# Batch 0 of a fused Fourier mixing and gated FFN kernel: even row sets summed as two 64-row tiles over half the columns

## The chip, the cores and the metric

The kernel runs on one core of one Trainium2 chip, in a single launch. The metric is the device time of that launch in microseconds (us), as a median of several runs. The engines are named as the profile names them: PE is TensorE's matmul and PEld its weight load, DVE is VectorE, ACT is ScalarE, POOL is GpSimd, and SP is SyncE, which here does nothing but issue DMA transfers. Each engine works through its own instructions in order.

## What is computed

```python
# x: (8, 3008, 256) float32; w_gate, w_val: (256, 1536); w_out: (1536, 256), given as float64
X = np.fft.fft(x, axis=1)              # along the sequence
X = np.fft.fft(X, axis=2)              # along the features
x = X.real.astype(np.float32).reshape(8 * 3008, 256)
gate = 1.0 / (1.0 + np.exp(-(x @ w_gate)))
val = x @ w_val
out = (gate * val @ w_out).astype(np.float32)
```

The real part of the two transforms is a cosine sum along the sequence times a cosine sum along the features, minus the same with sines. The feature transform is a fixed matrix, so the kernel multiplies it into w_gate and w_val once ("merge"), which gives the two halves G1 and G2. What is left per batch is a cosine sum pk and a sine sum qk along the sequence, for the outputs k = 0 to 1504. Row k of the output uses G1 pk + G2 qk, and row 3008 - k uses G1 pk - G2 qk.

## The kernel before, in words

**Rows and tables.** With S = 3008 and M = 1504, the input xf holds for each s from 0 to 767 the four rows s, S - s, M + s and M - s. s is p * 6 + q, where p is the partition (128 of them) and q = 0 to 5 is a "row set"; so the parity of s is the parity of q. The table stab holds the weighted cosines (t = 0) and sines (t = 1) of 2 pi s k / S in the same layout. Its columns are the even k from 0 to 752 (NE = 377 of them) and then the odd k (NO = 376); the two kinds of columns are "blk" 0 and 1.

**Folds.** `fold_ops` (L487) adds and subtracts the four rows of each s on DVE until each blk has 128 features for the cosine sum and 128 for the sine sum. For batch 0 it works in four slices of row sets, (0, 1), (2, 3), (4), (5) (L485), each with seven DVE instructions, L494 to L583.

**Sums.** `half` (L595), through `seq_group` (L680), makes one of the four groups (cosine or sine, blk 0 or 1). For each q a matmul with the folded rows as weights and 377 or 376 table columns adds into one of two PSUM banks: ev for even q, od for odd q. When all six are done, ACT copies ev to SBUF (L607), and `places` (L611) writes ev + od to the places of k and ev - od to those of M - k, one DVE instruction each (L613, L617). In the trace each float32 matmul is two instructions, so "x2" is one.

**The single feature column e.** Feature 128 has no partner in the fold. `e_sums` (L696) sums this column separately, for batch 0 during the start and for the other seven batches later from the tile x8. `e_load` (L684) fills x8 with one transfer for each of batches 1 to 7, issued at the main loop's steps 21 to 27; `e_fold` and `e_joint` use it at steps 36 to 44. Results go to the DRAM tile ed and come back as broadcast rows ek (`e_rows`, L755), from which ACT seeds the PSUM banks of the main loop (`seed`, L772). The ek row for steps 36 to 47 is issued at step 25.

**Weights.** Each of 18 pieces is loaded as float64 (`weight_load`, L328, 512 KB). ACT splits it (`weight_parts`, L382 and L383), DVE (`weight_join`, L392 to L395) and POOL (L397) put float32 numbers together, and `weight_use` either stores the piece or merges it: `merge` (L410) is four matmuls into one PSUM bank "ps" and two copies by ACT (L417, L418). Pieces 0 and 1, the first of w_gate and of w_val, have to be merged before the main loop.

**Main loop.** 576 steps (L1151) run over 8 batches, 6 chunks of up to 252 outputs k, and 12 blocks of 128 hidden features. `front_a` multiplies G1 with pk and `front_b` G2 with qk, into banks "pf"; ACT and DVE form the gates; POOL forms sums of gate blocks ("sf"), and `back` multiplies by the output weights into banks "po". Side work of later batches (loads, folds, tables) hangs on step numbers through lists such as `at(i, f)`. The table loads for batches 1 to 7 (`quarter_load`, L247) go to 32 partitions each.

**Order.** The order of instructions on each engine is the order in which the Python code issues them; nothing is reordered. All loads of the start go through SP's queue, in the order of L954 to L971. The start of batch 0 stands at L973 to L1015:

```python
    for q, f in zip(SLICES, fold_ops(0, 2), strict=True):
        f()
        e_(*{1: (0, 1), 5: (2, 3, 4, 5)}.get(q[-1], ()))
        sin[0][0](*{5: (3,)}.get(q[-1], ()))
        cos[0][0](*q)
        cos[1][0](*q)
        sin[0][0](*{1: (0, 1), 4: (2,), 5: (4, 5)}.get(q[-1], ()))
```

PSUM has eight banks: `bank(name)` takes one of three that rotate, `bank(name, i)` one of five named po0 to po4.

Of the kernel before, what the change touches and what calls it, by code (L numbers as in the profile page):

```python
# [8 lines left out]
F32 = mybir.dt.float32  # L9
# [3 lines left out]
ALU = mybir.AluOpType  # L13
# [40 lines left out]
NQ = 6  # L54
NP = 128
HP = 64
# [25 lines left out]
def kernel(  # L82
# [10 lines left out]
    nc = tc.nc  # L93
    B, _, _, _, D = xf.shape
    F = moe_w_gate.shape[1]
    P = 128
# [3 lines left out]
    NE = (M // 2) // 2 + 1  # L100
    NO = (M // 2) // 2
# [3 lines left out]
    CH = 252  # L105
    NB = 1 + max(b // 3 for b in PLACE)
    WC = 256
    HD = D // 2
# [23 lines left out]
    def mm(o, l, r, start, stop):  # L132
        nc.tensor.matmul(o, l, r, start=start, stop=stop, skip_group_check=True)  # L133
# [55 lines left out]
    ed = dram.tile([B, NK + 1], F32, name="ed")  # L189

    def load_rows(q, n):
        nc.sync.dma_start(out=X[0][0:NP, :, q : q + n], in_=xf[0, :, :, q : q + n])  # L192

    def load_table(t, q, n, lo=0, hi=NE + NO):
        nc.sync.dma_start(out=ST[t][0:NP, q : q + n, lo:hi], in_=stab[:, t, q : q + n, lo:hi])

    NQ4 = NE // 4 + 1
    TILES = [(g, par, par * HP + g * TB) for g in range(2) for par in range(2)]
# [178 lines left out]
    def weight_parts(j):  # L377

        if j in RAW:
            raw, ws = RAW[j], WS[j]  # L380
            lo, hi = raw[:, :, :, 0], raw[:, :, :, 1]
            nc.scalar.activation(ws, hi.bitcast(F32), AF.Abs)  # L382
            nc.scalar.activation(lo, lo.bitcast(U32), AF.Copy, scale=2.0 ** -29)  # L383

    def weight_join(j):
        if j not in RAW:
            return
        raw, ws = RAW.pop(j), WS[j]
# [8 lines left out]
        nc.gpsimd.tensor_tensor(wi, wi, lo, op=ALU.add)  # L397
# [5 lines left out]
    def weight_use(j):  # L403
        w, c = jobs[j]
        if w == 2:
            WO[c] = WS.pop(j)
        else:
            merge(WS.pop(j), w, c, (4, 2, 3)[next(turns) % 3] if j > 1 else None)

    def merge(ws, g, c, other):  # L410
        cs = slice(c * WC, (c + 1) * WC)
        ps = bank("ps", other)
# [179 lines left out]

    PQE = {}

    def half(b, w, d, blk, sn, other=None):  # L595


        c0, n = ((0, NE), (NE, NO))[blk]
        ev, od = [bank(name, other and other[i])[:, 0:n] for i, name in enumerate(("ev", "od"))]

        def sums(*qs):
            for q in sorted(qs, key=lambda q: q % 2):
                mm((ev, od)[q % 2], w(q), ST[int(sn)][0:NP, q, c0 : c0 + n], q < 2, q >= NQ - 2)

        def then():
            a = evp.tile([P, NE], F32, name="a", tag="a")[:, 0:n]
            nc.scalar.copy(a, ev)  # L607
            return lambda: places(d, blk, sn, a, od)
        return sums, then

    def places(d, blk, sn, ev, od, ends=(0, 1)):  # L611
        if 0 in ends:
            nc.vector.tensor_tensor(d[:, blk : blk + 2 * ev.shape[1] - 1 : 2], ev, od, op=ALU.add)  # L613
        lo, hi = (od, ev) if sn else (ev, od)
        top = M - blk
        if 1 in ends:
            nc.vector.tensor_tensor(d[:, top : top - 2 * NO + 1 : -2], lo[:, 0:NO], hi[:, 0:NO],  # L617
                                    op=ALU.subtract)
# [58 lines left out]
        for t in PQE[b]:  # L677
            nc.vector.memset(t[:, NK:], 0.0)

    def seq_group(b, blk, what, other=None):  # L680
        return half(b, lambda q: W[b, blk][what][:, q, :], PQE[b][what], blk, what == 1, other)


    def e_load(b):  # L684
        nc.sync.dma_start(out=x8[:, b - 1], in_=xf[b, :, :, :, HD : HD + 1])

    def e_fold():
        tt = nc.gpsimd.tensor_tensor
# [7 lines left out]
    def e_sums(m=B - 1):  # L696


        ps = bank("pe", NB - 1)
# [252 lines left out]
    nc.gpsimd.dma_start(out=zero, in_=nil)  # L952
    nc.scalar.dma_start(out=dt, in_=dtab.rearrange("(c p) d -> p c d", p=P))
    load_x(0)  # L954
    for j in range(2):
        weight_load(j)
    load_rows(0, 2)
    load_table(0, 0, 2)
    load_rows(2, 2)
    load_table(1, 0, 2, 0, NE)  # L960
    load_table(0, 2, 2)
    load_rows(4, 1)
    load_table(0, 4, 1)
# [12 lines left out]
    weight_parts(1)  # L976
    weight_join(0)
    weight_join(1)
# [5 lines left out]
    seq_start(0)  # L984

    cos = [seq_group(0, blk, 0, (2 * blk, 2 * blk + 1)) for blk in range(2)]
    e_, e_even = e_sums(1)
    sin = [seq_group(0, 0, 1)]
    for q, f in zip(SLICES, fold_ops(0, 2), strict=True):
        f()  # L990
        e_(*{1: (0, 1), 5: (2, 3, 4, 5)}.get(q[-1], ()))
        sin[0][0](*{5: (3,)}.get(q[-1], ()))
        cos[0][0](*q)
        cos[1][0](*q)
        sin[0][0](*{1: (0, 1), 4: (2,), 5: (4, 5)}.get(q[-1], ()))
    places_c = [cos[blk][1]() for blk in range(2)]
    weight_parts(2)
    weight_join(2)
    rest, *ends = e_even()
    rest()  # L1000
    for f in ends:
        f()
    for f in places_c:
        f()
    nc.scalar.copy(e0[0:1], E0[0][:, 0:CH])
    weight_parts(3)
    weight_join(3)
    sin.append(seq_group(0, 1, 1, (0, 1)))
    sin[1][0](*range(NQ))
    for j in range(KEEP, KEEP + 3):  # L1010
        weight_load(j)
    places_s = [group[1]() for group in sin]
    for f in places_s:
        f()
    e_rows(0)  # L1015

    per = NFT * len(chunks)
# [2 lines left out]
    def at(i, *fs):  # L1020
        side.setdefault(i, []).extend(fs)
# [224 lines left out]
```

## Time and profile before

| what | value |
|---|---|
| median of 3 runs | 1909.21 us (1908.49 to 1910.1) |
| the profiled execution | 1909.15 us, its span 1907.4 us |
| PE, DVE, POOL, ACT busy | 99%, 80%, 81%, 71% of the span |
| granted PE clock | 1.00 |
| DVE's folds of batch 0 | 10.18 to 24.61 us |
| first sum of the main loop (pf) | 33.05 us |
| last SP issue of an e_load | ends at 163.35 us |
| bytes moved by DMA | 109.33 MB, 315 GB/s in the first fortieth of the span |

A line of a timeline reads: start in us, time in us, engine, line of the code, operation, output<-inputs, shapes, number of instructions, and in brackets how long the engine had been idle and what released it. SPq is SP's queue; an SPq line is the time that the issue of a transfer took, not the transfer. A line of the table by windows gives, for each stretch, the busy time of PE, PEld, DVE, ACT and POOL with the number of instructions, then the granted clock, the mean busy share of the 16 DMA engines and what they moved in GB/s.

### The profile page before, as it was taken

How to read it: one execution, taken by the hardware profiler on the slowest of the kernel's cores; microseconds unless marked ns; L12 is line 12 of the kernel's file. 1: busy time of each engine (PE TensorE's matmuls, PEld its weight loads, DVE VectorE, ACT ScalarE, POOL GpSimd, SP SyncE). 2: the span in 40 equal slices, each digit the busy share in tenths (PEclk: the TensorE clock that was granted, in tenths of full speed). 3: DMA queues.
4: the chain of work that ended last, by engine and by line, in shares of the span. 5: the costliest groups of instructions: out<-in, count | busy, mean ns of one | idle time of the engine just before them, and what ended most of it. 6: DMA issues, size and time to landing. Idle time of an engine off the chain costs nothing.

```text
span 1907.4 us, 36057 instructions
## 1 busy us (share of the span) xinstructions
PE 1895.6 (99%) x11836; PEld 1756.6 (92%) x11836; DVE 1520.6 (80%) x3375; ACT 1353.2 (71%) x3235; POOL 1543.4 (81%) x2733
## 2 busy tenths in 40 slices
PE   8999999999999999999999999999999999999999
PEld 5788999999999999999999999999999999999998
DVE  7678888878979778897788878888788777977775
ACT  4777777777777777777777777677767777777775
POOL 2489879987999779997799878999789986877770
PEclk9999999999999999999999999999999999999999
DMA  8446221212022121211211212122120110010001
GB/s 315 120 134 80 71 89 51 72 33 81 21 64 54 31 87 32 62 41 37 89 39 48 45 39 81 40 52 58 30 74 17 36 37 15 15 25 17 15 18 30
DMA packets 197333, 109.33 MB, mean 57 GB/s; under 512 B 134823, under 2 KB 188818, under 8 KB 195354
## 3 DMA queue, kind: packets, MB, share of 16 engines
q1 hardware_dynamic: 196568, 106.50, 21.1%
q8 instruction: 95, 1.56, 0.3%
q14 instruction: 92, 0.75, 0.1%
q10 hardware_dynamic: 546, 0.51, 0.1%
q0 software_dynamic: 32, 0.00, 0.0%
HBM read 71.24 MB, written 47.87 MB: 62 GB/s over the span
## 4 chain that ended last, share of the span: by engine, by line
PE 94%; DMA 2%; SPq 1%; POOL 1%; ACT 1%; DVE 0%; issue 0%; ACTq 0%; POOLq 0%
PE pf L133 49%; PE po L133 41%; PE sum L133 2%; DMA rtab<-in_stab_dram 1%; PE ps L133 1%; POOL sf L824 1%; DMA st<-in_stab_dram 1%; SPq L206 1%; DMA raw<-in_moe_w_val_dram 0%; PE od L133 0%; POOL x L507 0%; SPq L192 0%; SPq L375 0%; PE pe L133 0%; PE ev L133 0%
## 5 line engine op out<-in xcount | busy, mean ns | idle before, releaser
L824 POOL TENSOR_TENSOR sf<-h,sf 128x168 f32<-128x168 f32 (+1 forms) x1104 | 621.0, 582 | 79.5 <-DVE h L818 75.9
L824 POOL TENSOR_TENSOR sf<-h 128x168 f32<-128x168 f32 (+1 forms) x920 | 519.3, 584 | 159.8 <-DVE h L818 158.0
L133 PE MATMUL pf<-qk,G 128*128 128x252 f32 (+1 forms) x2304 | 583.4, 376 | 0.9 <-ACT ae L787 0.8
L133 PE MATMUL pf<-pk,G 128*128 128x252 f32 (+1 forms) x2304 | 582.7, 376 | 0.0
L772 ACT ACTIVATE pf<-ek,ge 128x252 f32<-128x252 f32 (+1 forms) x1142 | 538.2, 471 | 23.2 <-DMA ge<-G 3.0
L133 PE MATMUL po<-sf,wf 128*128 128x168 f32 (+1 forms) x2944 | 508.3, 305 | 0.0
L787 ACT ACTIVATE ae<-pf 128x504 f32<-128x504 f32 (+1 forms) x576 | 338.8, 588 | 218.7 <-PE pf L133 217.2
L133 PEld LDWEIGHTS pf<-pk,G 128*128 128x128 f32 x2304 | 435.9, 190 | 53.3 <-ACT pf L772 1.5
L133 PE MATMUL po<-h,wf 128*128 128x168 f32 (+2 forms) x2584 | 461.3, 307 | 0.0
L133 PEld LDWEIGHTS po<-sf,wf 128*128 128x128 f32 x2944 | 453.4, 190 | 8.0
L818 DVE TENSOR_TENSOR h<-pf,z 128x252 f32<-128x252 f32 (+1 forms) x576 | 240.4, 417 | 274.0 <-ACT pf L815 270.5
L802 DVE TENSOR_TENSOR z<-ae,pf 128x504 f32<-128x504 f32 (+1 forms) x576 | 384.6, 668 | 83.1 <-ACT h L801 79.1
L908 DVE TENSOR_TENSOR c<-c 128x168 f32<-128x168 f32 (+1 forms) x920 | 438.7, 500 | 3.3
L133 PEld LDWEIGHTS pf<-qk,G 128*128 128x128 f32 x2304 | 410.6, 190 | 32.3 <-ACT ae L787 2.1
L133 PEld LDWEIGHTS po<-h,wf 128*128 128x128 f32 x2584 | 410.4, 190 | 17.8 <-issue 0.9
L801 ACT ACTIVATE h<-pf 128x252 f32<-128x252 f32 (+1 forms) x576 | 216.9, 376 | 146.3 <-PE pf L133 129.0
L815 ACT ACTIVATE pf<-z 128x252 f32<-128x252 f32 (+1 forms) x576 | 214.3, 372 | 116.4 <-DVE h L814 114.5
L814 DVE TENSOR_TENSOR h<-h,pf 128x252 f32<-128x252 f32 (+1 forms) x576 | 232.9, 404 | 0.0
L824 POOL TENSOR_TENSOR sf<-sf 128x168 f32<-128x168 f32 (+1 forms) x184 | 101.7, 553 | 14.4
L824 POOL TENSOR_TENSOR sf<-sf,h 128x168 f32<-128x168 f32 (+1 forms) x184 | 110.1, 598 | 0.0
L891 ACT COPY c<-po 128x504 f32<-128x504 f32 (+1 forms) x138 | 78.5, 569 | 0.0
L918 DVE STREAM_TRANSPOSE os<-c 128x256 f32<-128x256 f32 x188 | 76.5, 427 | 0.1
(158 smaller groups left out, 876.4 us busy)
## 6 DMA issues: line engine op xcount, KB each, us to landing
x<-xr SPq DMA_DIRECT2D x14, 1536.0 KB
out_dram<-os SPq DMA_DIRECT2D x376, 56.0 KB
xr<-in_xf_dram SPq DMA_DIRECT2D x105, 128.0 KB
x<-x SPq DMA_DIRECT2D x112, 96.0 KB
xr<-in_xf_dram SPq DMA_DIRECT2D x14, 384.0 KB
ek<-ed SPq DMA_DIRECT2D x40, 126.0 KB
out_dram<-os SPq DMA_DIRECT2D x288, 7.0 KB
xr<-in_xf_dram SPq DMA_DIRECT2D x21, 124.0 KB
```

Of the source, the lines that this page charges most:

```text
L133: nc.tensor.matmul(o, l, r, start=start, stop=stop, skip_group_check=True)
L772: nc.scalar.activation(PF[i][:, g], EK[i // NFT], AF.Copy, scale=ge[:, g, f : f + 1])
L787: nc.scalar.activation(AP[i], PF[i], AF.Copy, scale=2.0)
L801: nc.scalar.activation(H[p][:, fh, 0:n], PF[i][:, 0], AF.Sigmoid)
L802: nc.vector.tensor_tensor(z[:, :, ::-1], AP.pop(i), PF[i], op=ALU.subtract)
L814: nc.vector.tensor_tensor(h[:, fh, 0:n], h[:, fh, 0:n], pf[:, 1], op=ALU.mult)
L815: nc.scalar.activation(pf[:, 0], z[:, 0], AF.Sigmoid)
L818: nc.vector.tensor_tensor(h[:, fh, n:], pf[:, 0], z[:, 1], op=ALU.mult)
L824: nc.gpsimd.tensor_tensor(block(p, dst), block(p, a), block(p, b), op=(ALU.subtract, ALU.add)[op])
L891: (nc.vector.tensor_copy if t == 1 or t == 3 else nc.scalar.copy)(C[0][:, 3 * t * R : 3 * (t + 1) * R], PO[t][:, 0 : 3 * R])
L908: nc.vector.tensor_tensor(t[:, dst * R : (dst + 1) * R], *v, op=(ALU.subtract, ALU.add)[op])
L918: nc.vector.transpose(os_[0][0][:, s, 0:nb, h, :], t[:, c0 : c0 + nb * TB])
```

## The change

For even s the table columns mirror: the cosine of column 376 - j is plus or minus that of column j, with the sign of (-1)^(s/2), and odd k likewise. s/2 is 3p + q/2, so its parity alternates with the partition. The change puts the partitions of one parity into the lower 64 and those of the other into the upper 64: rows and tables of batch 0 are loaded as two strided transfers of 64 partitions each. An even row set is then summed as two matmuls of 64 rows, into two banks x and y, over 189 of the even k and 188 of the odd k only. When the sets are done, x + y gives one half of the columns and x - y the mirrored half ("unfolded", `join`: one ACT copy, two DVE instructions). Odd sets are summed over 128 rows and all columns as before. Of the sine tables of even sets only the 377 columns needed are loaded.

Since x8 must have the order of rows of the table, `e_load` becomes 48 transfers, one for each of 4 rows, 6 sets and 2 halves, each for all seven batches, eight at a time at steps 21 to 26. The loops that add them stand ahead of the one that adds `e_rows`, as before.

Weight piece 1 is loaded behind the cosine tables instead of ahead of the first rows. Its split, its join and its merge stand behind the folds and most sums. Piece 2 is loaded behind all tables.

```diff
     def load_rows(q, n):
-        nc.sync.dma_start(out=X[0][0:NP, :, q : q + n], in_=xf[0, :, :, q : q + n])
+        for h in range(2):
+            nc.sync.dma_start(out=X[0][h * HP : (h + 1) * HP, :, q : q + n], in_=xf[0, h ^ (q // 2 % 2) :: 2, :, q : q + n])
...
+        def even(q):
+            for blk, (lo, n, to) in enumerate(cols):
+                for h in range(2):
+                    rows = slice(h * HP, (h + 1) * HP)
+                    mm((x, y)[h][:, to : to + n], w[blk][rows, q], ST[what][rows, q, lo : lo + n],
+                       q == blk == 0, q == NQ - 2)
...
+            nc.vector.tensor_tensor(f[:, c0:c1], x[:, 0:NE], a, op=ALU.add)
...
+            nc.vector.tensor_tensor(f[:, 0 : 2 * c1].rearrange("p (b n) -> p b n", b=2)[:, :, c0 - 1 :: -1], *two,
+                                    op=ALU.subtract)
...
-    def e_load(b):
-        nc.sync.dma_start(out=x8[:, b - 1], in_=xf[b, :, :, :, HD : HD + 1])
+    def e_load(i):
+        r, q, h = i // (2 * NQ), i // 2 % NQ, i % 2
+        nc.sync.dma_start(out=x8[h * HP : (h + 1) * HP, :, r, q],
+                          in_=xf[1:, h ^ (q // 2 % 2) :: 2, r, q, HD].rearrange("b p -> p b"))
...
-    for j in range(2):
-        weight_load(j)
+    weight_load(0)
     load_rows(0, 2)
     load_table(0, 0, 2)
     load_rows(2, 2)
-    load_table(1, 0, 2, 0, NE)
+    load_sines(0)
+    load_rows(4, 1)
     load_table(0, 2, 2)
-    load_rows(4, 1)
+    load_rows(5, 1)
     load_table(0, 4, 1)
-    load_rows(5, 1)
-    weight_load(2)
-    load_table(1, 2, 2, 0, NE)
     load_table(0, 5, 1)
-    load_table(1, 4, 2, 0, NE)
-    load_table(1, 0, NQ, NE)
-    for j in (3, 5, 6, 8, 9, 4, 7):
+    weight_load(1)
+    load_sines(2)
+    load_sines(4)
+    for j in (2, 3, 5, 6, 8, 9, 4, 7):
         weight_load(j)
...
+    for q, f in zip(SLICES, folds, strict=True):
+        f()
+        for i in q:
+            (even, odd)[i % 2](i)
+        if q[0] == 0:
+            even_s(0)
+            odd_s(1, 0)
+            e_(0, 1)
+    pk = join(copy())
+    for blk in range(2):
+        pk(blk, 0)
+    HELD[1] = bank("ps")
+    od_s.append(bank("od"))
+    e_(2, 3, 4, 5)
+    odd_s(3, 0)
+    for q in (2, 4):
+        even_s(q)
+    odd_s(5, 0)
+    odd_s(1, 1)
+    weight_parts(1)
+    weight_join(1)
+    rest, last, end = e_even()
+    rest()
+    last()
+    for blk in range(2):
+        pk(blk, 1)
+    a = copy_s()
+    nc.scalar.copy(e0[0:1], E0[0][:, 0:CH])
+    weight_parts(2)
+    qk = join_s(a)
+    qk(0, 0)
+    weight_join(2)
     weight_use(1)
+    for q in (3, 5):
+        odd_s(q, 1)
+    qk(1, 0, 1)
     weight_parts(3)
     weight_join(3)
+    qk(0, 1)
+    end()
...
-    for b in range(1, B):
-        at(20 + b, lambda b=b: e_load(b))
+    for i in range(8 * NQ):
+        at(21 + i // 8, lambda i=i: e_load(i))
```

More of the change, by code (lines that the diff above doesn't have):

```diff
@@ L191, in load_rows, with load_sines @@
     def load_rows(q, n):
-        nc.sync.dma_start(out=X[0][0:NP, :, q : q + n], in_=xf[0, :, :, q : q + n])
+        for h in range(2):
+            nc.sync.dma_start(out=X[0][h * HP : (h + 1) * HP, :, q : q + n], in_=xf[0, h ^ (q // 2 % 2) :: 2, :, q : q + n])
     def load_table(t, q, n, lo=0, hi=NE + NO):
-        nc.sync.dma_start(out=ST[t][0:NP, q : q + n, lo:hi], in_=stab[:, t, q : q + n, lo:hi])
+        for h in range(2):
+            nc.sync.dma_start(out=ST[t][h * HP : (h + 1) * HP, q : q + n, lo:hi],
+                              in_=stab[h ^ (q // 2 % 2) :: 2, t, q : q + n, lo:hi])
+    def load_sines(q):
+        load_table(1, q, 1, NE // 2, NE + NO // 2)
+        load_table(1, q + 1, 1)
     NQ4 = NE // 4 + 1
@@ L407, in weight_use, with merge @@
         else:
-            merge(WS.pop(j), w, c, (4, 2, 3)[next(turns) % 3] if j > 1 else None)
-    def merge(ws, g, c, other):
+            merge(WS.pop(j), w, c, HELD.pop(j) if j in HELD else bank("ps", 2 + next(turns) % 3 if j else None))
+    HELD = {}
+    def merge(ws, g, c, ps):
         cs = slice(c * WC, (c + 1) * WC)
-        ps = bank("ps", other)
         for h in range(2):
@@ L593, with seq_sums, odd, copy @@
     PQE = {}
[L595 to L609, printed above, removed]
+    def seq_sums(what, x, y, od):
+        d, c0, c1 = PQE[0][what], NE // 2, NE + NO // 2
+        w = [W[0, blk][what] for blk in range(2)]
+        cols = (c0, NE - c0, 0), (NE, NO // 2, NE - c0)
+        F = (wf[:, 0].rearrange("p m n -> p (m n)"), None)[what]
+        def even(q):
+            for blk, (lo, n, to) in enumerate(cols):
+                for h in range(2):
+                    rows = slice(h * HP, (h + 1) * HP)
+                    mm((x, y)[h][:, to : to + n], w[blk][rows, q], ST[what][rows, q, lo : lo + n],
+                       q == blk == 0, q == NQ - 2)
+        def odd(q, *blks):
+            for blk in blks or range(2):
+                lo, n = ((0, NE), (NE, NO))[blk]
+                mm(od[blk][:, 0:n], w[blk][:, q], ST[what][0:NP, q, lo : lo + n], q == 1, q == NQ - 1)
+        def copy():
+            a = evp.tile([P, NE], F32, name="a", tag="a")
+            nc.scalar.copy(a, y[:, 0:NE])
+            return a
+        def join(a):
+            f = hp.tile([P, 6 * WC], F32, name="u", tag="h") if F is None else F
+            nc.vector.tensor_tensor(f[:, c0:c1], x[:, 0:NE], a, op=ALU.add)
+            two = [t[:, 1:NE].rearrange("p (b n) -> p b n", b=2) for t in (x, a)]
+            if what:
+                two.reverse()
+            nc.vector.tensor_tensor(f[:, 0 : 2 * c1].rearrange("p (b n) -> p b n", b=2)[:, :, c0 - 1 :: -1], *two,
+                                    op=ALU.subtract)
+            return lambda blk, *ends: places(d, blk, what == 1, f[:, blk * NE : NE + blk * NO],
+                                             od[blk][:, 0 : NE - blk], ends)
+        return even, odd, copy, join
     def places(d, blk, sn, ev, od, ends=(0, 1)):
@@ L678, in seq_start @@
             nc.vector.memset(t[:, NK:], 0.0)
-    def seq_group(b, blk, what, other=None):
-        return half(b, lambda q: W[b, blk][what][:, q, :], PQE[b][what], blk, what == 1, other)
-    def e_load(b):
-        nc.sync.dma_start(out=x8[:, b - 1], in_=xf[b, :, :, :, HD : HD + 1])
+    def e_load(i):
+        r, q, h = i // (2 * NQ), i // 2 % NQ, i % 2
+        nc.sync.dma_start(out=x8[h * HP : (h + 1) * HP, :, r, q],
+                          in_=xf[1:, h ^ (q // 2 % 2) :: 2, r, q, HD].rearrange("b p -> p b"))
     def e_fold():
@@ L696, in e_sums @@
     def e_sums(m=B - 1):
-        ps = bank("pe", NB - 1)
+        ps = bank("pe", NB - 1 if m > 1 else None)
         at_ = lambda blk, par: slice((2 * blk + par) * TB, (2 * blk + par) * TB + m)
@@ L975 @@
     weight_parts(0)
-    weight_parts(1)
     weight_join(0)
-    weight_join(1)
     warm = bank("warm", 2)
@@ L982 @@
     weight_use(0)
-    weight_use(1)
[L984 to L1005, printed above, removed]
+    seq_start(0)
+    folds = fold_ops(0, 2)
+    even, odd, copy, join = seq_sums(0, bank("u"), bank("u"), [bank("od", t) for t in range(2)])
+    e_, e_even = e_sums(1)
+    od_s = [bank("od", 4)]
+    even_s, odd_s, copy_s, join_s = seq_sums(1, bank("u", 2), bank("u", 3), od_s)
+    for q, f in zip(SLICES, folds, strict=True):
[30 more added lines that the diff above has]
+    weight_join(2)
+    weight_use(1)
+    for q in (3, 5):
+        odd_s(q, 1)
+    qk(1, 0, 1)
     weight_parts(3)
     weight_join(3)
-    sin.append(seq_group(0, 1, 1, (0, 1)))
-    sin[1][0](*range(NQ))
+    qk(0, 1)
+    end()
     for j in range(KEEP, KEEP + 3):
         weight_load(j)
-    places_s = [group[1]() for group in sin]
-    for f in places_s:
-        f()
     e_rows(0)
```

## The prediction

> **What bounds the kernel now.** The profiled execution took 1909.15 us: a span of 1907.4 us and 1.75 us around it; the median of the three runs shown is 1909.21 us, so the two can be used as one. I read the page's busy shares first, then PE's waits (us in total, times, longest), then the chain that ended last.
>
> ```profile
> PE 1895.6 (99%) x11836; PEld 1756.6 (92%) x11836; DVE 1520.6 (80%) x3375; ACT 1353.2 (71%) x3235; POOL 1543.4 (81%) x2733
> ```
>
> ```profile
> PE warm L133 <- DMA dt<-in_dtab_dram: 5.8, 1, 5.8
> PE ps L133 <- POOL raw L397: 1.6, 1, 1.6
> PE pf L133 <- ACT ae L787: 0.8, 2, 0.6
> ```
>
> PE is the bound almost to the end; all its waits together are 8.4 us, nearly all before 14 us. So a microsecond taken from the start-up should come off the whole, if nothing later is late. The chain (start, us, what) and PE's timeline show the start:
>
> ```profile
> 14.43 9.31 DMA st<-in_stab_dram
> ...
> 23.78 0.90 PE ev L133 x2
> ```
>
> ```profile
> 25.98 2.17 PE L133 MATMUL od<-st,x 128*128 128x377 f32 x6
> 27.99 0.80 PE L133 MATMUL ev<-st,x 128*128 128x377 f32 x2
> ...
> 31.15 2.06 PE L133 MATMUL od<-st,x 128*128 128x376 f32 x6
> 33.05 1.01 PE L133 MATMUL pf<-pk,G 128*128 128x252 f32 x4
> ```
>
> Batch 0's tables arrive while its sums run, and the first sum of the main loop (pf) starts at **33.05 us**. That is the number to forecast: from there PE goes on without a gap. DVE folds rows from 10.18 to 24.61 us without one either, so DMA, DVE and PE all stand close to the limit here.
>
> **Part 1: PE's work.** A full-height sum of 377 columns has a pitch of 0.63 us (27.99 to 28.62). Before, batch 0 has 24 of them. After, each of the six even row sets (three cosine, three sine) is two 64-row tiles of 189 and 188 columns. The trace has no 64-row sums. Upper bound: the tiles run one after the other, 1.27 us a set, as before. Lower bound: side by side, 0.63 us. The nearest row is the 32-row sum: 96 of 95 columns take 2.86 us, 30 ns each, where 168 full-height columns take 143 ns (1.43 us for ten), which makes 81 ns for 95. Row tiles do overlap; I take 0.63, so 6 x 0.63 = 3.8 us less. But merging the second weight piece, 1.73 us on PE, moves behind the folds, out of a time in which PE waits anyway.
>
> **Part 2: DVE, ACT, POOL.** The second piece's three DVE steps (7.84 to 10.24 us) no longer stand before the folds, nor does its POOL add, beside which a 128x4 step at L498 took 1.25 us instead of 0.16. That frees some 3 us of DVE, if rows are there. Added: two unfolding steps per sum on DVE, 4 x 0.53 = 2.1 us; gone: two copies on ACT, 0.47 us each. These lie beside DMA and PE in what follows.
>
> **Part 3: the loads, which decide.** Rows and tables of batch 0 now come as transfers to 64 partitions, twice as many, in a queue that the weights also use. The bytes fall (the sine tables of even sets lose half their columns), and the second piece's 0.52 MB goes behind the last cosine table. The question is the rate. Three stretches of loads to all 128 partitions and three to 32 partitions each (L247, four in a row to partitions 0 to 63, then four to 64 to 127):
>
> ```profile
> 20.00:24.00 4.00, 3.90 (x13) 2.05 (x12) 3.76 (x12) 0.75 (x2) 0.00 (x0) 1.00 1.05 376
> 24.00:28.00 4.00, 4.00 (x25) 1.64 (x25) 2.98 (x9) 2.29 (x5) 1.28 (x1) 1.00 1.07 382
> 28.00:30.00 2.00, 2.00 (x8) 1.24 (x7) 1.47 (x4) 0.87 (x2) 0.00 (x0) 1.00 1.05 388
> 139.00:142.00 3.00, 3.00 (x19) 2.84 (x18) 2.55 (x6) 2.59 (x7) 3.00 (x7) 1.00 1.07 217
> 142.00:145.00 3.00, 3.00 (x19) 2.84 (x18) 2.86 (x7) 2.15 (x6) 2.92 (x6) 1.00 1.09 213
> 145.00:148.00 3.00, 2.40 (x15) 2.06 (x14) 0.95 (x3) 1.46 (x5) 2.97 (x5) 1.00 1.11 209
> ```
>
> The last two columns are the DMA engines' busy share and GB/s. Both kinds keep the engines full (1.05 to 1.11), but the loads to 32 partitions move 213 GB/s and the others 382. The size of a piece is not the reason: the loads around 28 us also have pieces of some 1.5 KB (376 columns). So a transfer to one side of the 128 partitions goes at about half the rate. I take 213 for the 64-partition halves too; the other end is 382, if a half on each side can run at once.
>
> The Trainium skill, page "SBUF — State Buffer", section "Door 1: The DMA port swizzle (why [64,N] ≈ [32,N])", says that partitions 0 to 63 reach only 8 of 16 ports, measured at 196 GB/s for 1 MiB, and its section "Can I just issue two DMAs to hit both halves?" says that two transfers, one on each side, gained only 6%. The trace agrees for 32 partitions (213 GB/s); no run here shows 64. By the page's 196 x 1.06 = 208 GB/s the sum below would be some 0.8 us longer, an estimate from that page.
>
> Landing times after, from 5.03 us, when the first piece of weight is used (ACT L382, released by its DMA), in the order of the new queue. Rows 2 x 1.05 + 2 x 0.52 MB, cosines 2 x 0.77 + 2 x 0.39, sines 3 x 0.58: 7.19 MB at 213 GB/s are 33.8 us, and the second piece 0.52 MB at 380 another 1.4 us. Rows of sets 0 and 1 land at 9.9, of sets 2 and 3 at 18.5, of set 4 at 23.6, of set 5 at 29.7; the last cosine table at 33.3, the second piece at 34.7, the last sine table at **40.2**. Each fold waits for its rows (4.1, 4.1, 2.5, 2.5 us of DVE), each sum for its table, and what Parts 1 and 2 saved is spent waiting. The second piece's ACT (1.4), DVE (1.6) and POOL (1.3) steps end at 39.0. From 40.2 PE still has, in the order of the program, a sine sum of set 5 (0.63), one of set 1 (0.63), the merge (1.73) and two more sums (1.27): 4.3 us. The loop starts at 44.5, **11.4 us later**. Its third kind of sum needs the sine result 3.4 us into it, at 47.9; DVE has it at about 45.5.
>
> **Part 4: the loads of one feature column.** Seven e_load transfers become 48, of the same 21,504 elements of 4 bytes, on SP's queue, where the ek row of the next chunk is issued after 5 of 7 now, and after 40 of 48 then. SP's timeline before, and ACT's seed that reads the row:
>
> ```profile
> 146.53 11.06 SPq L685 DMA_DIRECT2D x<-in_xf_dram  x5
> 157.69 1.88 SPq L760 DMA_DIRECT2D ek<-ed  x1
> 159.61 3.74 SPq L685 DMA_DIRECT2D x<-in_xf_dram  x2
> ```
>
> ```profile
> 163.25 0.98 ACT L772 ACTIVATE pf<-ek,ge 128x252 f32<-128x252 f32 x2 [0.30 <-DMA ek<-ed]
> ```
>
> ACT already waits 0.30 us for ek, and PE reads what ACT seeds at once (164.28): no cover is left. Forty issues cost between 0.40 us each (L927's 0.36 and a gap of 0.04) and 0.69 (L163's 0.64 and a gap). The nearest are L247 (0.43 and gap: 0.47) and L685 itself where nothing held it (0.55 and gap: 0.60); I take 0.53: 40 x 0.53 = 21.2 us, ek is issued at 167.7 and lands some 1.8 us later (a ge row issued at 77.3 was used at 78.85; 0.3 for ek's size), at 169.5 instead of 163.2: **6.3 us** for ACT, and for PE behind it. Bounds: 1.1 and 12.7. All this is counted on the old clock; a later loop start moves both ends alike. The last eight, the "small" moves (L262) and the stores queue behind ek and have that stall as cover.
>
> **Sum.** 1909.15 + 11.4 + 6.3 = 1926.9, so **1927 us**.
>
> **Rivals.**
> - Half rate, but SP issues fast enough (0.37 us each or less: 163.2 - 1.8 - 146.5 over 40): 1920.6. Against it: no DMA row of this kind is that short. Chance 0.10.
> - Half rate, ek late, and PE slow besides. The warm-up sums at 5.79 take 435 ns each, the same shape 236 ns at 9.11. The new start-up leaves PE gaps of 3 to 4 us between folds, and the 4.3 us behind the last table could take twice as long: up to 4.3 us more, 1931. Against it: the granted clock shows 1.00 all along. Chance 0.12. The Trainium skill, page "TensorE: Matmul & The Clock Gate", Part 1, has such a halving after about 3.4 us of idling; the two rows speak for it, the profile's clock column doesn't.
> - Halves at the full 382 GB/s, ek late: the rows land at 7.8, the folds end at 22.2 instead of 24.6, PE's 8.8 us behind them make 31.1, ACT holds the first merges 0.5 us: 1.5 us earlier, 1907.7, and 6.3 for ek: 1914. Chance 0.10.
> - **The other side:** halves at full rate and issues of 0.37 us: 1907.7, faster. It needs both; by the first alone it decides where the last sine table lands by 28.8 us, which takes 321 GB/s. For it: engines could drift apart so that both sides are busy. Against it: L247's loads change sides too, and no microsecond of them exceeds 229. Chance 0.08.
> - The tiles don't overlap: in the forecast only the sums behind the last load count, and those are mostly odd sets; under 1 us. It would turn the faster rival into about 1911.
>
> **Chances and range.** The forecast with its bounds (201 to 229 GB/s, the lowest and highest microsecond of L247's loads: +2 and -2.4; issues: -5.2 and +6.4) has 0.60 and runs from 1920 to 1936. The range for 8 in 10 takes in part of the third rival and the second: 1912 to 1937. A measurement of this kernel tells about 0.2%, 3.8 us, from no change. Faster by more than that needs the last rival with more than I count for it: faster 0.06, within 0.07 (the rest of it and the edge of the third), slower 0.87.
>
> **What would show it.** Right: GB/s near 213 from 5 to 40 us with the engines full; DVE waiting for rows before each fold; PE's first pf sum near 44; 40 issues of e_load ahead of an ek for which ACT waits several us. Wrong: GB/s near 380 in the start-up, or a first pf sum before 33. A pair of 64-row sums at a pitch of 0.3 us would confirm Part 1 in any case.

## The result, and the profile after

The changed kernel takes **1938.7 us** (median of 6 runs, 1938.02 to 1939.93) beside 1909.78 us (6 runs, 1908.49 to 1910.1) for the kernel before: ratio 1.0153, 95% interval 1.014 to 1.0166. That is 28.9 us slower, where 17.8 were forecast, and just above the range. The profiled execution took 1938.9 us, 1.8 us more than its span of 1937.1 us; spans and starts are compared below.

First the busy shares and PE's longest wait in the kernel after (us in total, times, longest):

```profile
PE 1903.2 (98%) x11860; PEld 1762.1 (91%) x11860; DVE 1525.4 (79%) x3379; ACT 1352.3 (70%) x3233; POOL 1545.0 (80%) x2733
```

```profile
PE pf L133 <- ACT pf L799: 14.8, 2, 14.6
```

One wait of 14.6 us is new. It is half of the loss, and its line names ACT's seed, so the next question is what ACT waited for. PE is also *busy* for 7.6 us more although its sums were meant to take 3.8 us less, which says that some of its instructions ran slowly.

**The start.** The same three stretches as before (columns as there):

```profile
20.00:24.00 4.00, 3.39 (x19) 1.54 (x18) 3.70 (x7) 0.00 (x0) 0.00 (x0) 0.80 1.11 241
24.00:28.00 4.00, 1.28 (x8) 0.91 (x8) 2.47 (x7) 0.00 (x0) 0.00 (x0) 1.00 1.07 226
28.00:30.00 2.00, 2.00 (x6) 0.97 (x4) 0.38 (x1) 0.00 (x0) 0.00 (x0) 0.60 1.06 263
```

The DMA engines are as full as before (1.06 to 1.11), but they move 226 to 263 GB/s instead of 376 to 388. PE's timeline up to the first sum of the main loop:

```profile
36.58 0.87 PE L133 MATMUL od<-st,x 128*128 128x377 f32 x2 [1.32 <-DMA st<-in_stab_dram]
37.38 1.55 PE L133 MATMUL u<-st,x 64*128 64x189 f32 x16
38.87 1.53 PE L133 MATMUL od<-st,x 128*128 128x377 f32 x4
...
43.23 1.01 PE L133 MATMUL pf<-pk,G 128*128 128x252 f32 x4
```

The loop (pf) starts at 43.23 instead of 33.05 us: **10.2 us later**. The second line is the new kind of sum: 16 records are the eight 64-row tiles of two even sets, and the next line starts 1.49 us behind it, so a set costs 0.75 us.

**The feature column.** SP's queue, and then the chain that ended last where it passes the awaited row (start, us, what):

```profile
157.84 27.96 SPq L711 DMA_DIRECT2D x<-in_xf_dram  x40
186.26 0.36 SPq L787 DMA_DIRECT2D ek<-ed  x1
```

```profile
186.26 3.13 DMA ek<-ed
...
189.48 0.48 ACT pf L799
```

Forty issues take 28.0 us, 0.70 us each: the chain shows most as 0.63 us with 0.04 us behind it, and a few that take longer (1.12 and 1.16 us). ek is issued at 186.26, lands 3.13 us later, ACT seeds at 189.48, and PE goes on:

```profile
190.51 2.05 PE L133 MATMUL pf<-pk,G 128*128 128x252 f32 x4 [14.61 <-ACT pf L799]
```

That sum takes 2.05 us where it takes 1.01 elsewhere. The table by windows around the stall gives the reason in its granted clock, the third number from the end:

```profile
180.00:190.00 10.00, 0.00 (x0) 0.00 (x0) 0.00 (x0) 0.49 (x2) 0.00 (x0) 0.50 0.41 16
190.00:196.00 6.00, 5.49 (x17) 5.05 (x18) 4.19 (x10) 2.79 (x7) 4.60 (x8) 0.53 0.25 9
196.00:200.00 4.00, 4.00 (x23) 3.73 (x23) 2.30 (x6) 2.49 (x6) 3.84 (x10) 1.00 0.28 60
```

The clock is at half in the stall and stays there for about 5 us of renewed work. Just ahead of the stall PE is 11.3 us later than in the kernel before (a pf sum at 174.89 instead of 163.58); at the first pe sum behind it, it is 28.7 us later (209.06 instead of 180.35). So the stretch costs 17.4 us: 14.6 waiting and 2.8 at half clock.

**Ledger**, from the places of the same PE instructions in the two traces:

| stretch | lost, us |
|---|---|
| to the first pf sum | 10.2 |
| steps 1 to 5 (waits of 0.8, 0.2, 0.2 for ACT and others), less 0.4 given back at 148 us | 1.1 |
| the wait for ek | 14.6 |
| half clock behind it | 2.8 |
| all the rest, to the last po sum (1895.51 and 1925.08) | 0.9 |
| sum | 29.6 |

### The profile page after: what moved, and what is told of

The parts are those of the page before. It is cut to its first block, busy times and chain, and to the rows that moved or that the text cites. A ratio compares the mean times of both kernels' runs of the same rounds, so it can differ in the third digit from the quotient of the medians.

```text
span 1937.1 us, 36183 instructions
## 1 busy us (share of the span) xinstructions
PE 1903.2 (98%) x11860; PEld 1762.1 (91%) x11860; DVE 1525.4 (79%) x3379; ACT 1352.3 (70%) x3233; POOL 1545.0 (80%) x2733
## 3 DMA queue, kind: packets, MB, share of 16 engines
q1 hardware_dynamic: 196712, 105.93, 21.2%
## 4 chain that ended last, share of the span: by engine, by line
PE 90%; DMA 3%; SPq 3%; DVE 1%; POOL 1%; ACT 1%; issue 0%; ACTq 0%; POOLq 0%
PE pf L133 47%; PE po L133 40%; PE sum L133 2%; SPq L711 1%; DMA st<-in_stab_dram 1%; DMA rtab<-in_stab_dram 1%; POOL sf L851 1%; DMA x<-in_xf_dram 1%; SPq L213 1%; PE ps L133 0%; ACT pf L799 0%; SPq L254 0%; DMA ge<-G 0%; DMA out_dram<-os 0%; POOL x L515 0%
## 5 line engine op out<-in xcount | busy, mean ns | idle before, releaser
L133 PE MATMUL pf<-pk,G 128*128 128x252 f32 (+1 forms) x2304 | 584.1, 376 | 15.6 <-ACT pf L799 14.8
L133 PEld LDWEIGHTS pf<-pk,G 128*128 128x128 f32 x2304 | 436.0, 190 | 70.3 <-ACT pf L799 17.8
L935 DVE TENSOR_TENSOR c<-c 128x168 f32<-128x168 f32 (+1 forms) x920 | 445.7, 508 | 3.3
L133 PEld LDWEIGHTS po<-h,wf 128*128 128x128 f32 x2584 | 410.9, 190 | 17.9 <-issue 0.9
```

What stands on the lines that cost most here:

```text
L935: nc.vector.tensor_tensor(t[:, dst * R : (dst + 1) * R], *v, op=(ALU.subtract, ALU.add)[op])
```

## The experiments

Theory: two independent losses, both from loads that were cut. Halves of 64 partitions go at 60% of the rate in the start; 48 issues of e_load hold up ek, and PE falls to half clock behind that. Rivals: the *number* of transfers is what costs (in the start and with e_load); ek's issue alone, wherever it stands, decides; the half clock is only a sign of the stall.

### The 48 loads alone, and ek in front of them

**e2**: the kernel before, with e_load's 48 transfers and nothing else of the change (rows in their natural order).

```diff
-    def e_load(b):
-        nc.sync.dma_start(out=x8[:, b - 1], in_=xf[b, :, :, :, HD : HD + 1])
+    def e_load(i):
+        r, q, h = i // (2 * NQ), i // 2 % NQ, i % 2
+        nc.sync.dma_start(out=x8[h * HP : (h + 1) * HP, :, r, q],
+                          in_=xf[1:, h * HP : (h + 1) * HP, r, q, HD].rearrange("b p -> p b"))
...
```

> The kernel before with one edit: its seven e_load transfers become 48, for 64 partitions each, in the natural order of rows. Start-up and sums are untouched. Theory (the queue): 40 issues of 0.67 us ahead of ek make PE wait 14 to 15 us and lose about 3 us at half clock: 1926 to 1928 us. Rival (the stall needs the later start or the new order of rows): no more than 1 us, 1909 to 1911.

Measured: 1926.57 us, ratio 1.0092 (1.0078 to 1.0105), 17.9 us slower, with the loop starting at 32.87 us. SP's queue shows the same pitch as in the kernel after (27.43 us for 40), and PE the same wait (14.0 us):

```profile
146.31 27.43 SPq L686 DMA_DIRECT2D x<-in_xf_dram  x40
```

So this part of the loss needs nothing else of the change.

**e3**: the kernel before, each of the seven e_load transfers cut into two halves of 64 partitions: 14 issues.

```diff
-        nc.sync.dma_start(out=x8[:, b - 1], in_=xf[b, :, :, :, HD : HD + 1])
+        for h in range(2):
+            ps = slice(h * HP, (h + 1) * HP)
+            nc.sync.dma_start(out=x8[ps, b - 1], in_=xf[b, ps, :, :, HD : HD + 1])
```

> The kernel before with 14 e_load transfers instead of 7: each batch in two of 64 partitions, 1536 elements each. Same 4-byte elements, same halves as in the 48, but few issues. Theory (what an issue costs is the cause): 10 issues ahead of ek instead of 5; the engines need about 1 us for the elements of each, more than the 0.67 us of an issue, so ek comes as before: 1908 to 1911 us, PE's wait there under 1 us. Rival (scattered 4-byte elements into one half of the partitions are the cause): PE waits several us for ACT's seed, 1914 or more.

Measured: 1909.01 us, ratio 0.9999 (0.9989 to 1.0008).

```profile
146.24 10.68 SPq L687 DMA_DIRECT2D x<-in_xf_dram  x10
```

Ten issues of half the size take 10.68 us, as long as five whole ones did (11.06). Halves cost e_load nothing; cutting it into the 48 does.

**e1**: the kernel after, with the ek row of steps 36 to 47 issued at step 20, ahead of all 48.

```diff
-        at(i - (8 if i == i0 else 11), lambda i=i: e_rows(i))
+        at(i - (8 if i == i0 else 16 if i == 3 * i0 else 11), lambda i=i: e_rows(i))
```

> The changed kernel with one line moved: the ek row for steps 36 to 47 is issued at step 20, ahead of the 48 e_load issues instead of behind 40 of them. Theory (the queue): PE's stall of 14.6 us for ACT's seed goes, and with it the 2.8 us that PE then loses at a clock of 0.50. What is late next is e_fold on POOL, which needs all of x8: 48 issues of 0.67 us end some 6 us after POOL wants it, of which PE may see 0 to 6 us. 1921 to 1927 us. Rival (the seed is late for another cause, such as the later start of the main loop or a slow DMA): the stall stays and the time with it, about 1938.

Measured: 1931.3 us, ratio 1.0117 (1.0103 to 1.013): 7.4 us better than the kernel after (6.3 by the runs of the kernel before beside each), where 12 to 18 were expected. The 14.6 us are gone, but the queue's delay comes back later:

```profile
157.38 34.34 SPq L711 DMA_DIRECT2D x<-in_xf_dram  x48
```

```profile
DVE er L740 <- DMA out_dram<-os: 11.6, 1, 11.6
...
PE pf L133 <- ACT ae L814: 4.2, 2, 4.1
```

The "small" moves and the stores stand behind the 48 on SP. DVE's er step waits 11.6 us for a store to free its buffer, ACT waits for DVE and PE for ACT (4.1 us); PE also waits 3.2 us for POOL's x, which waited 7.4 us for "small". The clock's mean over 188 to 212 us is 0.86. The two waits of PE, 3.2 and 4.1 us, and some 3 us at half clock behind them are about the 10 us by which the gain of 7.4 falls short of the 17.4 that the stall had cost. The prediction's sentence that these transfers "have that stall as cover" holds: without the stall they have none.

**e6**: the kernel after, with 60 matmuls that nothing needs added on PE in front of the seed that waits for ek.

```diff
+        for j in range(60 if i == 3 * NFT else 0):
+            mm(PF[i][:, j % 2, 0:HD], dt[:, 0, 0:P], dt[:, 0, 0:HD], True, True)
```

> The changed kernel with 60 extra sums of 128 columns on PE (results overwritten) just ahead of the seed of step 36, so that PE works while ACT waits for ek. Work is only added. Theory (PE at 0.50 of its clock behind the stall costs 2.8 us of its own): the extra sums take some 13 us that PE would have idled, the clock stays at 1.00, the time falls by 2 to 3 us, to 1935 to 1937 us. Rival (the low clock after the stall costs nothing, because other engines are late too): no change or slower, 1938.7 or more.

Measured: 1936.81 us, ratio 1.0144 (1.0127 to 1.0161): 1.9 us *less* than the kernel after, with 13.66 us of work added. The two kernels ran on different chips; by the runs of the kernel before beside each, the losses are 27.6 and 28.9 us, so the gain is 1.3 to 1.9 us. In the trace ek was issued 1.1 us later than in the kernel after (187.36), and the pe sum behind the stall still starts 1.4 us earlier (207.67): some 2.5 us are won behind ek. The windows:

```profile
176.00:188.00 12.00, 12.00 (x110) 12.00 (x109) 0.57 (x2) 0.00 (x0) 2.87 (x6) 1.00 0.37 4
188.00:196.00 8.00, 6.72 (x39) 6.01 (x39) 4.08 (x10) 3.75 (x10) 3.58 (x6) 1.00 0.38 20
```

The clock stays at 1.00, and pf sums behind the stall take 1.01 to 1.12 us. So the low clock follows PE's idling and has a price of its own. The Trainium skill, page "TensorE: Matmul & The Clock Gate", Part 1, says that PE drops to half clock after a window of some 3.4 us without work and needs about as long a busy one to come back. The traces agree in kind, but not with one fixed time: by the mean clock of single microseconds, half clock begins 2.7 us into the stall of the kernel after and 5.3 us into that of e2, and full clock is back 5.1 and 5.0 us after PE's work resumes.

### The loads of the start

**e7**: the kernel after, but e_load as seven whole transfers, from a copy of x whose rows lie in the changed order (made outside the kernel; its permuting is not in the time).

```diff
-    for i in range(8 * NQ):
-        at(21 + i // 8, lambda i=i: e_load(i))
+    for b in range(1, B):
+        at(20 + b, lambda b=b: e_load(b))
```

> The changed kernel with the halves of rows and tables as they are, but e_load as seven transfers to 128 partitions, from a copy of xf that lies in DRAM in the new order of rows. Theory (two losses that add up): what stays is the start-up, 43.2 us instead of 33.05 to the first pf sum and 1 to 1.5 us lost by ACT right behind it: 1919.5 to 1921.5 us. Rival (the losses share something, such as the clock or the queue): not within 2 us of that.

Measured: 1921.31 us, ratio 1.0064 (1.0049 to 1.0079), loop start at 43.52 us. That is 12.1 us above the kernel before; with e2's 17.9 it makes 30.0, beside 28.9 for the whole change. So the two losses add up.

**e4**: the kernel before, with rows and tables of batch 0 in two halves of 64 partitions.

```diff
-        nc.sync.dma_start(out=X[0][0:NP, :, q : q + n], in_=xf[0, :, :, q : q + n])
+        for h in range(2):
+            ps = slice(h * HP, (h + 1) * HP)
+            nc.sync.dma_start(out=X[0][ps, :, q : q + n], in_=xf[0, ps, :, q : q + n])
...
```

> The kernel before with one edit: rows and tables of batch 0 are loaded as two transfers of 64 partitions each; same bytes, same order, all sums as before. Theory (one side of the partitions goes at some 235 GB/s, as in the start-up after the change): 7.8 MB take 33 us instead of 20, the last sine table lands at about 41 us, the main loop starts at 41 to 43 us instead of 33: 1917 to 1920 us. Rival (the later start comes from the merge and the sums behind the folds, not from the rate): GB/s near 380, 1909 to 1911.

Measured: 1924.95 us, ratio 1.0084 (1.007 to 1.0097): the direction as expected, the size missed. The rate is that of the kernel after (228 to 234 GB/s between 20 and 30 us):

```profile
20.00:24.00 4.00, 2.19 (x7) 0.76 (x5) 3.69 (x6) 0.00 (x0) 0.00 (x0) 1.00 1.06 234
```

But the full sine tables still have to pass at it, PE waits 7.0 and 2.3 us for tables, and its clock is at 0.5 in part of the start; the loop starts at 47.51 us.

**e9** cuts the same loads in two as well, but by columns, so that each transfer still goes to all 128 partitions. **e8** cuts them in three by partitions: 32 to 95, across the middle, then 0 to 31 and 96 to 127. The edits of the row load, e9's and then e8's (that of the tables is alike, by its columns and by its partitions):

```diff
-        nc.sync.dma_start(out=X[0][0:NP, :, q : q + n], in_=xf[0, :, :, q : q + n])
+        for r in (slice(0, 2), slice(2, 4)):
+            nc.sync.dma_start(out=X[0][0:NP, r, q : q + n], in_=xf[0, :, r, q : q + n])
```

```diff
-        nc.sync.dma_start(out=X[0][0:NP, :, q : q + n], in_=xf[0, :, :, q : q + n])
+        for ps in (slice(HP // 2, 3 * HP // 2), slice(0, HP // 2), slice(3 * HP // 2, NP)):
+            nc.sync.dma_start(out=X[0][ps, :, q : q + n], in_=xf[0, ps, :, q : q + n])
```

> The kernel before with rows and tables in two transfers each again, but cut by columns: both to all 128 partitions. As many transfers as in e4. Theory (it is the side of the partitions, not the number of transfers): GB/s near 385 as before, the main loop starts at 32.5 to 34 us, 1908.5 to 1910.5 us. Rival (the number of transfers or their issue is what slowed e4): 1915 us or more.

> The kernel before with rows and tables in three transfers each: partitions 32 to 95, then 0 to 31, then 96 to 127. The first has 64 partitions like the halves of e4, but lies across the middle. Theory (a transfer to one side, 0 to 63 or 64 to 127, goes at some 235 GB/s; one across both at full rate): half of the bytes at 385 and half at 235, so 280 to 300 GB/s in the start-up, the main loop starts at 38 to 42 us instead of e4's 47.5, time 1914 to 1919 us. Rival (fewer partitions for each transfer are slower, wherever they lie, or more transfers are): as slow as e4 or slower, 1925 us or more, GB/s near 235.

Measured: e9 1910.42 us, ratio 1.0007 (0.9998 to 1.0016), loop start 34.09, at the edge of the expected 32.5 to 34. e8 1918.57 us, ratio 1.005 (1.0035 to 1.0065), loop start 42.76, just behind the expected 38 to 42. Two stretches of each, e9 first:

```profile
20.00:24.00 4.00, 3.53 (x12) 1.71 (x10) 3.76 (x12) 0.91 (x3) 0.00 (x0) 1.00 1.08 355
24.00:28.00 4.00, 3.50 (x22) 1.47 (x23) 2.17 (x8) 2.11 (x5) 1.28 (x1) 1.00 1.10 333
```

```profile
20.00:24.00 4.00, 2.42 (x7) 1.14 (x6) 2.08 (x4) 0.00 (x0) 0.00 (x0) 0.73 1.06 241
24.00:28.00 4.00, 4.00 (x8) 2.21 (x7) 2.47 (x7) 0.00 (x0) 0.00 (x0) 0.50 1.08 257
```

Twice as many transfers cost next to nothing (333 to 355 GB/s) while each reaches both sides. Transfers that reach one side are slow, and a third of the transfers going across the middle helps only in part (237 to 315 GB/s in its stretches between 10 and 30 us). e8's transfers go to 64 and 32 partitions, no more than e4's, and there are more of them; still its loop starts 4.8 us before e4's. So which partitions a transfer reaches decides, not how many transfers there are.

### Without both losses: where the intended gain goes

**e5**: the kernel after with whole loads throughout: rows, tables and e_load go to all 128 partitions, from copies of x and of the table in the changed order, made outside the kernel.

```diff
-        for h in range(2):
-            nc.sync.dma_start(out=X[0][h * HP : (h + 1) * HP, :, q : q + n], in_=xf[0, h ^ (q // 2 % 2) :: 2, :, q : q + n])
+        nc.sync.dma_start(out=X[0][0:NP, :, q : q + n], in_=xs[0, :, :, q : q + n])
```

> The changed kernel with its new sums and its new order, but rows and tables come as transfers to 128 partitions each, from copies of xf and of the table that lie in DRAM in the new order of rows, and e_load is seven transfers again. What is left of the change is the tiles, the unfolding and the moved second piece. Theory: both losses came from the transfers alone, folds end near 22 us, the main loop starts at 31 to 32 us, ek is no later than before: 1907 to 1908.5 us. Rival (the tiles or the unfolding cost what they save): 1909 to 1913.

Measured: 1909.18 us, ratio 1.0001 (0.9992 to 1.001): no change. The loop does start 1.5 us earlier (31.57 us, loads at 385 GB/s), and then PE waits:

```profile
44.09 0.69 PE L135 MATMUL pf<-pk,G 128*128 128x252 f32 x2 [1.60 <-ACT G L425]
```

ACT's order explains it: the copy of G stands behind an ACT step (L839) that had waited 2.81 us for DVE's product of the first gate. DVE had been without a pause since 28 us (22.6 busy of the 25 us from 20 to 45, before 20.6): the unfolding and the second piece's join now stand behind the folds, and DVE starts the first gate's product at 40.88 us, 0.7 later than before although the loop started earlier. One step is also longer: that for the feature column (er, at 35.48) takes 1.46 us, most of it while POOL's add runs (35.24 to 36.54), where its like takes 0.53.

Four edits of e5 test that. All four move the places of the mirrored ends of the cosine sum to step 3, and e12 does only this:

```diff
-    for blk in range(2):
-        pk(blk, 1)
...
+    gap[3] = [lambda: pk(0, 1), lambda: pk(1, 1)]
```

e10 moves the end of the feature column's sums, `e_rows(0)` and the last places of the sine sum too:

```diff
-    qk(0, 1)
-    end()
...
-    e_rows(0)
...
+    at(0, lambda: qk(0, 1))
+    gap[2] = [end]
+    at(2, lambda: e_rows(0))
```

e13 moves the join of the fourth weight piece behind step 0's gate, beside e12's edit:

```diff
-    weight_join(3)
...
+    join[1] = [lambda: weight_join(3)]
```

e11 is e13 with that join entered at a place of the list that is never read (`join[0]`). Its kernel so left the join of the fourth weight piece out altogether, not moved as its expectation says, so part of the weights is wrong and 1.5 us of DVE's work is gone.

> As e5 (the change with whole loads), with DVE work that is not needed at once moved into steps 0 to 3 of the main loop: the upper halves of pk and one of qk, and the last step of batch 0's feature column with its store and its ek row. Theory (e5's 1.5 us came back as a wait of PE for ACT's copies, which wait for a DVE that is full from 22 to 41 us): the wait of 1.6 us shrinks below 0.5, the time is 1907.3 to 1908.3 us, about 1 us below e5. Rival (ACT itself or the weights' DMA is the limit there): PE's wait and the time stay as in e5, 1909.

> The kernel with whole loads, and in front of the first gate DVE has two things fewer to do: the places of the mirrored ends of the cosine sum (two instructions, about 1.1 us; made at step 3 instead) and the join of the fourth weight piece (three, 1.5 us; made behind step 0's gate). Theory (what the whole loads gained is given back because DVE is full until the first gate): the gate's first product comes 1.5 us or more earlier than 40.88 us, PE's wait of 1.60 us for G falls to 0.5 or less, and the time is 1907.5 to 1908.5, about 1 us under the kernel before, with the first sum of the main loop at or before 31.6 us. Rival (DVE was not what held it: ACT's order or the merges' chain give the gain back in any case): PE waits as long in sum over steps 0 to 5, and the time stays at 1909 to 1910.5.

> The kernel with whole loads, with only the places of the mirrored ends of the cosine sum (two DVE instructions, about 1.1 us) moved behind step 3. Theory (DVE is full until the first gate): the gate's first product comes about 1 us earlier than 40.88 us, PE's wait for G falls from 1.60 us to about 0.6, the time is 1908 to 1909. Rival: the join of the fourth piece or ACT takes the place, the wait stays over 1.2 us, 1909 to 1910.

> The kernel with whole loads, complete, with the places of the mirrored ends of the cosine sum at step 3 and the join of the fourth weight piece behind step 0's gate (where the kernel before left it out altogether, and PE's wait for G was gone). Theory (the order on DVE in front of the first gate is what gives the gain of whole loads back): the join's 1.5 us costs nothing behind the gate, the first gate's product comes before 39.5 us, PE waits less than 0.5 us for G or ps in steps 0 to 5, and from the first to the last sum of the main loop it is no longer than in the kernel before (1862.5 us); 1907.3 to 1908.3. Rival (DVE's load, not its order): the join, its POOL add and the merge behind it make PE wait 1 us or more at step 1, and the time is 1908.5 to 1909.5.

| kernel | first pf sum | first pf to last po | first gate's product behind the first pf | time, us | ratio to before (95%) |
|---|---|---|---|---|---|
| before | 33.05 | 1862.5 | 7.1 | 1909.2 | |
| e5 | 31.57 | 1864.2 | 9.3 | 1909.18 | 1.0001 (0.9992 to 1.001) |
| e12 | 32.54 | 1862.9 | 8.5 | 1908.26 | 0.9997 (0.9988 to 1.0006) |
| e11 | 31.43 | 1863.0 | 7.1 | 1907.57 | 0.9993 (0.9984 to 1.0002) |
| e10 | 31.51 | 1865.9 | 8.5 | 1910.68 | 1.0007 (0.9998 to 1.0016) |
| e13 | 31.41 | 1870.3 | 7.1 | 1915.23 | 1.0031 (1.0019 to 1.0044) |

The times of e11 and e12 came out in the range of the theory. Counted from the first pf sum, the gate comes earlier by about what was taken from DVE (2.2 us for 2.6 in e11, 0.8 for 1.1 in e12), PE's wait for G falls to 0.85 us (e12) and to nothing that the trace lists (e11), and the loop is shorter than e5's by 1.2 to 1.3 us. On the clock e12's gate is no earlier, 41.07 beside 40.88 us, though its expectation had said so: its profiled execution started the loop 1.0 us later than e5's. And neither kernel differs from the kernel before by more than the measurement can tell, and e11 isn't a complete kernel. e10 and e13 missed. In e10 the wait for G is gone and another comes, 2.0 us for ACT's ae, with PE at half clock behind it until about 45.3 us (1.7 us more); that the feature column's tiles hold ae's buffers longer is an argument from the code that no run tested. e13 shows the cost of a step that is moved past its due time:

```profile
43.02 3.78 PE L135 MATMUL ps<-wqk,dt 128*128 128x256 f32 x8 [5.47 <-POOL wqk L403]
```

The fourth piece's merge stands on PE right behind the third's; in e11 it runs at 37.4 us. In e13 the join ends at 41.5 us and POOL's add behind it at 43.0, so PE waits 5.47 us, and it comes out of that at half clock (3.78 us for a merge that takes 1.89 elsewhere). So DVE is full in front of the first gate, and this join, one of the steps there, is needed just then and cannot be put off. With whole loads the change is worth about nothing here, and no version tried beats the kernel before beyond doubt.

## Why the prediction was wrong in size

- **What bounds the kernel** was read rightly: a later loop start is kept to the end (10.2 us at 43 us, and 1.1 more by 170 us).
- **Part 3, the rate, was right**, and the size nearly: the halves went at 221 to 241 GB/s between 10 and 28 us, not 213, DVE waited for its rows before each of the four folds (10.9 us in all), and the loop started 10.2 us later, not 11.4. That this is so close is partly luck, since two errors offset each other. The rows came at 11.6, 19.6, 24.2 and 29.6 us, up to 1.7 us later than forecast, but the tables behind them came sooner: from 28 to 36 us, where the second weight piece, a load to all partitions, passes among them, 259 to 291 GB/s were moved. PE's last wait for a table ends at 36.58 us, where the last table was forecast for 40.2. And PE had 6.65 us of sums behind that wait, not 4.3, since the even sets 2 and 4 (1.5 us) and one more sum of an odd set were still to do. The estimate from the Trainium skill, page "SBUF — State Buffer" (208 GB/s, 0.8 us longer), was further off: e4 has 228 to 234 in its middle. The Trainium skill's point there, in the section "Can I just issue two DMAs to hit both halves?", that two transfers, one on each side, gain little over one, stands. Neither trace comes near 385 while only halves are loaded.
- **Part 4 is the step that failed: "I take 0.53: 40 x 0.53 = 21.2 us, ek is issued at 167.7 and lands some 1.8 us later".** The mechanism was right and both terms were too small. An issue took 0.70 us, just above the upper bound of 0.69 that L163 gave, and 40 of them 28.4 us up to ek's issue: 7.2 more. ek landed 3.13 us after its issue: 1.3 more. 6.3 + 7.2 + 1.3 = 14.8, beside the 14.6 that PE waited. That is 8.3 of the 12 us by which the whole forecast was short; the rest is the half clock (2.8), which stands in no term of the sum, and 2.0 of smaller losses, less the 1.2 by which the start came out better. Both terms could have been read better from before. The row picked for the pitch, L685's 0.55 us, was one whole load at 159.61; another of the same line, issued at 146.53 and followed at 147.18, has 0.65 with its gap. And the landing was taken from a ge row at a quiet time, where the same ek transfer stood in the same trace: its issue ended at 159.57 and ACT had it at 163.2, 3.6 us later (in the kernel after 2.9 us, counted in the same way).
- **The half clock was weighed at the wrong place.** The second rival looked for it in the start. There the clock did fall (0.50 in 15 to 20 us), but from 36.58 us, where PE decides, its sums ran at full speed (clock 1.00 from 36 to 43.3 us). It cost 2.8 us behind the stall in Part 4, a wait that the forecast itself had made longer than the 3 to 4 us it feared in the start, without asking the same question there.
- **Part 1** was nearly right: tiles do overlap, at 0.75 us a set, between the bounds of 0.63 (side by side, as forecast) and 1.27 (one after the other).
- **Part 2, "these lie beside DMA and PE", was right only because DMA was slow.** With whole loads, e5, DVE has no such room: the first gate came later and 1.6 us of PE came back. The rival with halves at full rate, which put a start 1.5 us earlier at 1907.7, had the start right (31.57) and the time wrong (1909.18) for that reason.

## What to carry to other kernels

Cut a load by columns or by rows of the source, and keep all 128 partitions in each transfer; where the DMA engines are full, a cut by partitions costs the rate even when transfers to the two sides follow each other. When one issue becomes many on an in-order queue, price them by the dearest row of that queue and not the nearest-looking one, then look at every small transfer behind them, and at who waits for each. And ask of each stall that you forecast whether it is long enough to slow the clock of the engine that waits.

## What the runs showed of the hardware

- Loads of 448 elements of 4 bytes to 64 partitions pass SP's queue at 0.63 us and a gap each (0.69 to 0.72 us on the mean in e2, the kernel after and e6), though five loads of 3072 elements take 11.06 us and ten of 1536 take 10.68, both 0.7 ns an element. By that rate 448 elements would be 0.31 us. So the whole loads look held by what the queue takes in, and the cut ones by the issue itself (a whole load at a free moment took 0.55 us); this is argued from the sizes, and no run tested it. The 48 also differ from the 14 of e3 in pattern (each takes one row of all seven batches), which no run set apart from their number.
- Alternating halves of 64 partitions move 221 to 241 GB/s with the engines full (the kernel after, 10 to 28 us; e4 228 to 234), whole loads 385 (e5), column halves 333 to 366 (e9), and with half of the bytes across the middle 237 to 315 (e8).
- After 14.6 us without work PE ran at half clock for about 5 us more. Work that nobody needs, put in its place, made the kernel 1.3 to 1.9 us faster. Far shorter waits did the same: one of 2.0 us in e10, one of 3.2 us in e1 (half clock began 2.5 and 2.8 us after PE stopped). A wait of 1.6 us left the clock at 1.00 in the kernel before and in e5.
- Four fp32 64-row matmuls of 189 and 188 columns take 0.75 us as two tiles, 1.7 times as fast as the 1.27 us that they would take one after the other (an estimate from the full-height pitch of 0.63 us; no run has them so).
